# First pairs of an attention: half of one rotation moved to Pool, one to DVE, idle products added, SyncE's order fixed

## The chip, the cores and the metric

The kernel runs on one core of a Trainium2 chip. The core has a matrix engine (PE, with PEld for its weight loads), a vector engine (DVE), a scalar engine (ACT), a general engine (POOL), a queue engine that only issues transfers (SP, SyncE), and 16 DMA engines that carry the transfers. The metric is the device time of one launch in microseconds (us). Before the change it is 1183.55 us, the median of three runs (1183.39 to 1185.93).

## The reference

Three stages follow one another, all in float32:

```
# 1: attention, 2 batches x 8 heads, 576 positions, 64 wide
q, k = rotate(q), rotate(k)                 # x1*cos - x2*sin, x1*sin + x2*cos
attn = softmax(q @ k.T / sqrt(64));  x = attn @ v
# 2: top-1 experts over the 1152 rows of x (512 wide), 8 experts, 1024 hidden
idx = argmax(cosine(x, expert_emb) / tau);  x = gate * relu(x @ w1[idx]) @ w2[idx]
# 3: 8 dense experts, mixed by a matrix P that is normalized 8 times in turn
out = sum_e P[:, e] * (relu(x @ w1[e]) @ w2[e])
```

## The kernel before

The attention works on eight pairs of heads. A pair's q and k lie in one tile `r` (128 partitions: head j = 0 on partitions 0 to 63, head j = 1 on the rest; index x = 0 is q, x = 1 is k). A pair goes through five stations:

- `load_pair` loads `r`, `load_values` loads the values `vr`; both are issued by SP.
- `rotate` multiplies `r` by the table `tb` and adds the two halves: two instructions, on DVE or Pool.
- `split_pair` cuts q or k in a high and a low part: ACT writes the high part into `hl`, Pool subtracts to get the low part, and SP copies both by DMA into `qd` (four transfers of 144 KB) or `kd` (four of 288 KB), where the two parts of one head lie on 128 partitions.
- `scores` multiplies `kd` with `qd` on PE; DVE takes the row maximum `nb`, ACT the exponential `p`.
- `turn`, `values`, `rows` transpose `p`, multiply it with the values and turn the result.

The loop runs in steps k = 0 to 88. A step does the scores of one block of 120 rows (five blocks a head, ten steps a pair), so pair i is first needed at step 10 i. In step 10 (i - 1) + 3 pair i's q is split, in step 10 (i - 1) + 5 its k; only for pair 1 are these steps 8 and 7. The first pair is not split: its scores come straight from the tile `first`, which takes 64 partitions, that is one head, at a time. Its rotation is cut in six instructions a head by `rotate_first`: all of k, then q's columns 0 to 239, then the rest. Before the loop, 30 products of a tile `wz` of ones (`keep_warm`) run on PE; nothing uses them.

SP also issues the first expert's weights for stage 2: `fetch(raw1, w1a, ...)` stands at the head of step 15 and `fetch(raw2, w2a, ...)` at the head of step 55, four transfers of 512 KB each.

`with tc.manual_schedule(engines=ORDERED)` keeps the order of the code on PE, DVE, ACT and Pool. SP is not in `ORDERED` before, so its order is chosen by the scheduler. SP's transfers use eight semaphores in turn: each transfer from the ninth on waits until the one eight places ahead of it has landed. All of them go through one hardware queue (q1).

Of the kernel before, what the change touches and what calls it, by code (L numbers as in the profile page):

```python
# [36 lines left out]
ORDERED = {mybir.EngineType.PE, mybir.EngineType.DVE, mybir.EngineType.Activation, mybir.EngineType.Pool}  # L37
# [10 lines left out]
def fused_kernel(ctx, tc, qk, vv, tab, cst, emb, tau, w1a, w2a, wg, w1b, w2b, out):  # L48
    nc = tc.nc
    V, A, G, T = nc.vector, nc.scalar, nc.gpsimd, nc.tensor  # L50
# [9 lines left out]
    def bank(tag, bufs, name, shape=(128, 512)):  # L60
        return ps[0].tile(list(shape), F32, tag=tag, bufs=bufs, name=name)
# [13 lines left out]
    def fetch(raws, src, n, e, cond=None):  # L75

        ei = slice(e, e + 1) if isinstance(e, int) else bass.ds(e, 1)
        for i, raw in enumerate(raws):
            nc.sync.dma_start(out=raw.rearrange("p (g c) -> p g c", g=n // 128),
                              in_=src[ei, i * n:(i + 1) * n, :].rearrange("o (g p) c -> p (o g) c", p=128),  # L80
                              **({} if cond is None else dict(cond=cond)))
# [4 lines left out]
    cs = rt.tile([128, C_END], F32, name="cs")  # L86
# [12 lines left out]
        for x in (1, 0):  # L99
            nc.sync.dma_start(out=first[half, x], in_=qk[0, 0, half, x])  # L100
    nc.sync.dma_start(out=io, in_=cst[:, :256])
    nc.sync.dma_start(out=cs, in_=cst[:, 256:])
    em = at.tile([E, DM], F32, name="em")
    nc.sync.dma_start(out=em, in_=emb)
    taut = at.tile([128, 1], F32, name="taut")
    nc.sync.dma_start(out=taut, in_=tau.to_broadcast([128, 1]))

    def inv_norm(dst, sq, tmp):

# [21 lines left out]
    def embeddings():  # L131

        esq = at.tile([E, DM], F32, name="esq")
        es = at.tile([E, 4], F32, name="es")
        yield V.tensor_copy(uo[:, :128], cs[:, COLS["u"]])
        yield V.tensor_copy(uo[:, 128:], ones)
        yield A.activation(esq, em, AF.Square, accum_out=es[:, 0:1])
        yield V.reciprocal(taut, taut)
        yield from inv_norm(es[:, 1:2], es[:, 0:1], es[:, 2:3])
        yield V.tensor_tensor(es[:, 1:2], es[:, 1:2], taut[:E], op=ALU.mult)  # L140
        yield V.tensor_scalar_mul(em, em, es[:, 1:2])
        yield
        yield
        p = bank("t", 2, "pe_")
        for c in range(NP):
            T.transpose(p[:, c * E:(c + 1) * E], em[:, c * 128:(c + 1) * 128], ident[:E, :E])
        pv = p[:, :NP * E].rearrange("p (c e) -> p c e", e=E)
        for j in range(2):
            half = slice(j * 64, (j + 1) * 64)
            yield V.tensor_copy(enb[half, :, j, :], pv[half])  # L150
# [14 lines left out]
    wz = at.tile([128, 512], BF16, name="wz")  # L165
    V.memset(wz, 1.0)

    def load_pair(i):
        b, pr = divmod(i, NP)
        r = first  # L170
        if i > 0:
            r = at.tile([128, 2, 2, S], F32, tag="r", bufs=2, name="r")
            nc.sync.dma_start(out=r, in_=qk[b, pr])
        ops[i] = dict(r=r)

    def load_values(i):
        b, pr = divmod(i, NP)
        vr = ops["v", i] = at.tile([QT, NQ, 2, D], F32, tag="vr", bufs=3, name="vr")
        G.memset(vr[96:QT, 4], 0.0)
        nc.sync.dma_start(out=vr[:, 0:4].rearrange("p t h d -> p t (h d)"),  # L180
                          in_=vv[b, pr, 0:480].rearrange("(t p) d -> p t d", p=QT))
        nc.sync.dma_start(out=vr[0:96, 4].rearrange("p h d -> p (h d)"), in_=vv[b, pr, 480:S])
# [6 lines left out]
    def rotate(i, x, eng, rows=slice(0, 128), cols=slice(0, S)):  # L189
        r = ops[i]["r"][rows, x][:, :, cols]  # L190
        eng.tensor_tensor(r, r, tb[rows][:, :, cols], op=ALU.mult)
        eng.tensor_tensor(r[:, 0], r[:, 0], r[:, 1], op=ALU.add)

    def rotate_first(j):

        rows, c, rest = slice(j * 64, (j + 1) * 64), slice(0, 2 * QT), slice(2 * QT, S)
        yield rotate(0, 1, V, rows)
        yield rotate(0, 0, V, rows, c)
        yield rotate(0, 0, V, rows, rest)

    def split_pair(i, x):

# [31 lines left out]
    def exps(n, t, s, nb):  # L234
        i, j = divmod(n, 2)
        m = TW[t]
        A.activation(ppad[n % 2][:m, t, :S].rearrange("p (h n) -> p h n", h=2), s[:m, :, :HS], AF.Exp,  # L237
                     bias=nb[:m], scale=1.0, accum_out=sums[:m, i, t, j:j + 1])
# [28 lines left out]
    def gather_pair(i):  # L267
        A.activation(upad[i % 2][:, :S].rearrange("p (h n) -> p h n", h=2), ops["o", i][:, :, :HS], AF.Copy)
# [9 lines left out]
    def keep_warm(w, n):  # L278

        p = bank("t", 2, "warm")  # L280
        for _ in range(n):
            T.matmul(p, w[:, :128], w[:, :512], start=True, stop=True)
# [149 lines left out]
    def squares(b):  # L432
        for c in range(NQ):
            sq = tmp("sq", [QT, DM], BF16) if (b, c) == (0, 0) else ops["sq"]
            ops["sq"] = sq
            yield A.activation(sq, ops["x", b][:, c], AF.Square, accum_out=nsq[:, b, c:c + 1])
# [37 lines left out]
        V.tensor_copy(idx[:, 1], ig)  # L474

    pairs = B * NP
    for i in range(2):
        load_pair(i)
        load_values(i)
    trickle = embeddings()  # L480
    heads = 2 * pairs

    ahead = {0: 2, 3: 0, 5: 1}
    last = pairs - 1
    with tc.manual_schedule(engines=ORDERED):
        waiting, out_rows, squared = None, None, iter(())
        keep_warm(wz, 30)
        second = rotate_first(1)
        for _ in rotate_first(0):
            pass  # L490
        for k in range(NQ * heads + 9):
            n, t = divmod(k, NQ)
            nt, kt = divmod(k - 6, NQ)
            iv, kv = divmod(k - 12, 2 * NQ)
            if waiting is not None:
                exps(*waiting)
                waiting = None
            if k in (1, 2, 3):
                next(second, None)
            if k >= 7:  # L500
                for _ in range(2 if k < 40 else 1):
                    next(trickle, None)
            if k == 15:
                fetch(raw1, w1a, 128, 0)
            if k == 55:
                fetch(raw2, w2a, 256, 0)
            if out_rows is not None:
                rows_out(*out_rows)
                if out_rows[:2] == (NP - 1, 1):
                    trickle, squared = route_half(0), squares(0)  # L510
                out_rows = None
            next(squared, None)
            if n < heads:
                waiting = (n, t) + scores(n, t)

            if iv >= last:
                kv *= 2
            if 0 <= iv <= last and kv == 9 + (iv == last):
                gather_pair(iv)
            if 0 <= nt < heads:  # L520
                if kt == 0:
                    ops["ph", nt] = at.tile([128, NQ, S], F32, tag="ph", bufs=4, name="ph")[:QT]
                    turn(nt, -1)
                turn(nt, kt)
            if 0 <= iv <= last and kv % 2 == 0 and kv < 2 * NQ:
                if kv == 0:
                    ops["o", iv] = bank("o", 1, "o", (128, 2, 512))
                values(iv, kv // 2)
            if iv == last and kv == 12:
                keep_warm(ops[last]["k"][:, 0, 0], 8)  # L530
                logits_first(last)
                parts = [rows(last, x) for x in range(2)]
            elif 0 < iv <= last and k % (2 * NQ) in (2, 3):
                out_rows = rows((k - 22) // (2 * NQ), k % (2 * NQ) - 2)
            i = k // (2 * NQ) + 1
            if k < 2 * NQ:

                part = {0: 2, 7: 1, 8: 0}.get(k)
                if k == 5:
                    rotate(1, 1, V)  # L540
            else:
                part = ahead.get(k % (2 * NQ))
            if part is not None and i < pairs:
                if part < 2:
                    split_pair(i, part)
                else:
                    room(i)
                    rotate(i, 0, G)
                    if i > 1:
                        rotate(i, 1, G)  # L550
                        load_values(i)
                    if i + 1 < pairs:
                        load_pair(i + 1)
        routes = route_half(1)
        for _ in range(5):
            next(routes)
        for x in parts:
            rows_out(*x)
        next(routes)
# [647 lines left out]
```

## Time and profile before

| what | us |
|---|---|
| median of three runs | 1183.55 |
| the profiled execution's own time | 1185.82 |
| its span, first to last instruction | 1183.70 |
| PE busy in the span | 1146.0 (97%) |
| DVE, ACT, POOL busy | 838.5, 513.9, 144.5 |

The profiled execution took 2.12 us outside its span, and 2.27 us more than the median. The attention's scores begin at 10.88 us, the second pair's at 41.44, the third's at 59.37; the attention's last block ends near 186. From the second pair on PE is nearly always busy.

Times in rows are us from the start of the span. The granted clock of PE (PEclk) is 1.00 at 2.4 GHz and 0.50 at 1.2 GHz. Line numbers are those of the kernel before; the changed file's lines are 3 higher in the functions and the loop.

### The profile page before, as it was taken

Reading aid. Unit: us, or ns where it says so; the run is one execution under the profiler, and the core shown is the slowest. Engines: PE = TensorE matmul, PEld = TensorE weight load, DVE = VectorE, ACT = ScalarE, POOL = GpSimd, SP = SyncE. Lnnn points to the kernel's source line nnn. Section 1 sums busy time; section 2 is a strip of 40 time slices with the busy share of each in tenths; the row PEclk is TensorE's granted clock in tenths of the full one; section 3 lists DMA queues with packets and bytes.
Section 4 is the critical chain, followed back from the end, with each engine's and each line's share of the span. In section 5 each row is a group of like instructions: output and inputs, shape, how many; then the busy total and the mean of one; then the engine's idle time right before and its main releaser. Section 6 shows DMA issues by size and latency. Waiting matters only on the chain.

```text
span 1183.7 us, 17171 instructions
## 1 busy us (share of the span) xinstructions
PE 1146.0 (97%) x6658; PEld 981.4 (83%) x6658; DVE 838.5 (71%) x1293; ACT 513.9 (43%) x788; POOL 144.5 (12%) x95
## 2 busy tenths in 40 slices
PE   8999998999998889999999999999999999999998
PEld 4677776788886768899989998899989998989997
DVE  6776776899996456776676667666766676667665
ACT  2565754788885344323332333333333333333330
POOL 2657403133231200000000000000000000000000
PEclk7799998999999789999999999999999999999999
DMA  7788524355285401111111111111111111111102
GB/s 209 206 239 207 133 54 131 125 177 214 84 293 185 125 19 36 54 54 36 36 54 54 37 36 54 54 36 37 55 54 36 38 53 54 37 40 50 36 1 81
DMA packets 75187, 103.90 MB, mean 88 GB/s; under 512 B 5400, under 2 KB 45336, under 8 KB 74208
## 3 DMA queue, kind: packets, MB, share of 16 engines
q1 hardware_dynamic: 72160, 94.13, 26.7%
q0 software_dynamic: 2368, 7.60, 1.9%
q8 instruction: 53, 0.87, 0.3%
q10 hardware_dynamic: 576, 1.05, 0.2%
q14 instruction: 30, 0.25, 0.1%
HBM read 111.35 MB, written 8.39 MB: 101 GB/s over the span
## 4 chain that ended last, share of the span: by engine, by line
PE 64%; DVE 1%; DMA 1%; issue 1%; ACT 1%; SPq 0%; POOLq 0%
PE o L1062 34%; PE d L1026 29%; DMA g<-yd 1%; PE o L970 0%; DVE yq L897 0%; DMA yd<-y,idx 0%; ACT yq L894 0%; DVE yt L942 0%; PE d L922 0%; PE o L1001 0%; ACT h L1051 0%; DVE st L1041 0%; DVE w L859 0%; ACT w L858 0%; SPq L910 0%
## 5 line engine op out<-in xcount | busy, mean ns | idle before, releaser
L1062 PE MATMUL o<-w,h 128*128 128x512 f32 x1728 | 433.6, 393 | 0.7 <-ACT acc L1066 0.7
L1026 PEld LDWEIGHTS d<-yq,w 128*128 128x128 f32 x2688 | 381.7, 189 | 20.5 <-ACT st L1038 1.0
L1026 PE MATMUL d<-yq,w 128*128 128x288 f32 x2688 | 395.4, 296 | 1.3 <-ACT st L1038 0.7
L1062 PEld LDWEIGHTS o<-w,h 128*128 128x128 f32 x1728 | 312.8, 188 | 55.4 <-ACT acc L1066 1.1
L1073 DVE SCALAR_TENSOR_TENSOR acc<-o,P,acc 128x512 f32<-128x512 f32 x252 | 189.1, 750 | 160.0 <-PE o L1062 160.0
L1051 ACT ACTIVATE h<-st 128x576 fp32r<-128x576 f32 x96 | 65.8, 686 | 223.2 <-DVE st L1041 223.2
L1038 ACT ACTIVATE st<-d 128x576 f32<-128x576 f32 x96 | 62.7, 653 | 221.6 <-PE d L1026 221.6
L572 DVE TENSOR_TENSOR wlo<-raw,whi 128x2048 fp32r<-128x2048 f32 x56 | 127.8, 2288 | 15.8 <-ACT whi L579 15.5
L579 ACT ACTIVATE whi<-raw 128x2048 fp32r<-128x2048 f32 x52 | 99.9, 1920 | 10.9 <-PE h L607 3.5
L1041 DVE TENSOR_TENSOR st<-st,d 128x576 f32<-128x576 f32 x96 | 72.1, 751 | 41.0 <-PE d L1026 41.0
L237 ACT ACTIVATE p<-s,nb 120x576 f32<-120x576 f32 (+1 forms) x80 | 59.1, 739 | 62.5 <-DVE nb L231 52.5
L231 DVE TENSOR_REDUCE nb<-s 120x1 f32<-120x576 f32 (+1 forms) x80 | 60.2, 754 | 35.2 <-PE s L228 18.9
L804 ACT ACTIVATE w<-raw 128x512 fp32r<-128x512 f32 (+1 forms) x128 | 73.3, 573 | 17.3 <-DVE raw L842 14.0
L805 DVE TENSOR_TENSOR w<-raw,w 128x512 fp32r<-128x512 f32 (+1 forms) x128 | 78.9, 617 | 0.0
L1052 DVE SCALAR_TENSOR_TENSOR h<-st,h 128x576 fp32r<-128x576 f32 x96 | 72.0, 750 | 4.8 <-ACT h L1051 4.7
L228 PE MATMUL s<-kd,qd 128*120 128x288 f32 x280 | 55.7, 322 | 3.9 <-DMA qd<-hl 2.6
L228 PEld LDWEIGHTS s<-kd,qd 128*120 128x120 f32 x280 | 39.3, 182 | 16.6 <-issue 10.2
L251 PE MATMUL pt<-io,p 120*120 120x120 f32 x320 | 48.6, 276 | 1.4 <-DVE ph L257 0.3
L634 PE MATMUL y<-whi,hh 128*128 128x512 f32 x112 | 45.7, 408 | 2.2 <-ACT hh L624 2.2
L264 PE MATMUL o<-ph,vr 120*64 120x288 f32 x320 | 47.4, 418 | 0.0
L634 PE MATMUL y<-wlo,hh 128*128 128x512 f32 x112 | 44.2, 394 | 0.0
L257 DVE COPY ph<-pt 120x480 f32<-120x480 f32 x64 | 41.5, 649 | 2.9 <-PE pt L251 2.6
(245 smaller groups left out, 1123.4 us busy)
## 6 DMA issues: line engine op xcount, KB each, us to landing
raw<-w1a SPq DMA_DIRECT2D x56, 512.0 KB
raw<-w2a SPq DMA_DIRECT2D x56, 512.0 KB
raw<-w1b SPq DMA_DIRECT2D x64, 256.0 KB
raw<-w2b SPq DMA_DIRECT2D x32, 512.0 KB
r<-qk SPq DMA_DIRECT2D x7, 1152.0 KB
kd<-hl SPq DMA_DIRECT2D x28, 288.0 KB
qd<-hl SPq DMA_DIRECT2D x28, 144.0 KB
g<-yd SPq DMA_DIRECT2D x4, 576.0 KB
```

The lines of the kernel that those rows point to most:

```text
L228: T.matmul(s[:m, h, :HS], qd[:, j, t * QT:t * QT + m], kd[:, j, x, h * HS:(h + 1) * HS], start=(x == 0), stop=(x == 1))
L572: V.tensor_tensor(lo, raw, hi, op=ALU.subtract)
L579: A.activation(hi, raw, AF.Copy)
L634: T.matmul(p, a[:, kk], b, start=(k == 0 and n == 0), stop=(k == KF - 1 and n == 2))
L804: A.activation(hi, src, Copy)
L805: V.tensor_tensor(lo, src, hi, op=ALU.subtract)
L1026: T.matmul(d[1][:, q, :QW], wv[:, wx, which, k], yq[yx][:, YQ[p], k, q * QW:(q + 1) * QW], start=new and k == 0 and (wx, yx) == (0, 0), st ...
L1041: V.tensor_tensor(halves(st[x]), halves(st[x]), mid(d), op=ALU.add)
L1051: A.activation(hi, src, AF.Relu)
L1052: V.scalar_tensor_tensor(lo, src, 0.0, hi, op0=ALU.max, op1=ALU.subtract)
L1062: T.matmul(d, hs[n][:, r, hx, t * 128:(t + 1) * 128], w2[n][:, wx, r], start=(r == 0 and (hx, wx) == (0, 0)), stop=(r == 1 and hx == 1))
L1073: V.scalar_tensor_tensor(a, d, p, a, op0=ALU.mult, op1=ALU.add)
```

## The change

Four edits, all in the attention:

- The second head of the first pair is rotated by Pool instead of by DVE, whole and ahead of the loop (before, DVE did it in steps 1 to 3). Pool's rotation of pair 1's q goes to DVE: it rotates pair 1's k in step 4 and q in step 5. Pair 1's k is then split in step 6, its q in step 7.
- Pair 1's load stands ahead of the constants `cs`, `em`, `taut` and of the values.
- 28 products of `wz` instead of 30 run before the loop, and three more follow each of the steps 0 to 5 and two each of the steps 6 to 9.
- SP is added to the engines that keep the code's order.

```diff
-    nc.sync.dma_start(out=cs, in_=cst[:, 256:])
     em = at.tile([E, DM], F32, name="em")
-    nc.sync.dma_start(out=em, in_=emb)
     taut = at.tile([128, 1], F32, name="taut")
-    nc.sync.dma_start(out=taut, in_=tau.to_broadcast([128, 1]))
+
+    def load_constants():
+        nc.sync.dma_start(out=cs, in_=cst[:, 256:])
+        nc.sync.dma_start(out=em, in_=emb)
+        nc.sync.dma_start(out=taut, in_=tau.to_broadcast([128, 1]))
...
-    def rotate_first(j):
+    def rotate_first(j, eng):
         rows, c, rest = slice(j * 64, (j + 1) * 64), slice(0, 2 * QT), slice(2 * QT, S)
-        yield rotate(0, 1, V, rows)
-        yield rotate(0, 0, V, rows, c)
-        yield rotate(0, 0, V, rows, rest)
+        rotate(0, 1, eng, rows)
+        rotate(0, 0, eng, rows, c)
+        rotate(0, 0, eng, rows, rest)
...
-    for i in range(2):
-        load_pair(i)
-        load_values(i)
+    load_pair(0)
+    load_pair(1)
+    load_values(0)
+    load_constants()
+    load_values(1)
...
-    with tc.manual_schedule(engines=ORDERED):
+    with tc.manual_schedule(engines=ORDERED | {mybir.EngineType.SP}):
-        keep_warm(wz, 30)
-        second = rotate_first(1)
-        for _ in rotate_first(0):
-            pass
+        keep_warm(wz, 28)
+        rotate_first(0, V)
+        rotate_first(1, G)
...
-            if k in (1, 2, 3):
-                next(second, None)
...
-                part = {0: 2, 7: 1, 8: 0}.get(k)
-                if k == 5:
-                    rotate(1, 1, V)
+                part = {0: 2, 6: 1, 7: 0}.get(k)
+                if k in (4, 5):
+                    rotate(1, 5 - k, V)
+                keep_warm(wz, 3 if k < 6 else 2)
...
                     room(i)
-                    rotate(i, 0, G)
                     if i > 1:
+                        rotate(i, 0, G)
                         rotate(i, 1, G)
```

On SP, from pair 1's split (the first `kd` and `qd`) to pair 2's (the second), before:

```order
L215 DMA kd<-hl 64x2x576 x4
L213 DMA qd<-hl 64x576 x4
L173 DMA r<-qk 128x2304
L79 DMA raw_74<-w1a 128x1024
L79 DMA raw_75<-w1a 128x1024 x2
L213 DMA qd<-hl 64x576 x4
L215 DMA kd<-hl 64x2x576 x4
```

and now:

```order
L218 DMA kd<-hl 64x2x576 x4
L216 DMA qd<-hl 64x576 x4
L183 DMA vr<-vv 120x4x128
L185 DMA vr<-vv 96x128
L176 DMA r<-qk 128x2304
L216 DMA qd<-hl 64x576 x4
L79 DMA raw_74<-w1a 128x1024 x2
L79 DMA raw_75<-w1a 128x1024 x2
L218 DMA kd<-hl 64x2x576 x4
```

The first expert's `w1a`, of which one transfer was issued ahead of pair 1's `kd` and three ahead of pair 2's `qd`, now goes out as four transfers between pair 2's `qd` and its `kd`. On SP, around the split of pair 6 (steps 53 to 55), before:

```order
L329 DMA xd<-x 120x3x128
L213 DMA qd<-hl 64x576 x4
L329 DMA xd<-x 120x128
L332 DMA xd<-x 96x128
L215 DMA kd<-hl 64x2x576 x4
```

and now:

```order
L332 DMA xd<-x 120x3x128
L216 DMA qd<-hl 64x576 x4
L332 DMA xd<-x 120x128
L335 DMA xd<-x 96x128
L79 DMA raw_76<-w2a 128x2x512 x2
L79 DMA raw_77<-w2a 128x2x512 x2
L218 DMA kd<-hl 64x2x576 x4
```

The four `w2a` transfers, which before stood in twos ahead of the `qd` of pairs 3 and 4, now stand between `qd` and `kd` of pair 6. On DVE, from the end of the first head's rotation to the first copy of a transposed block, now:

```order
L195 TENSOR_TENSOR first<-first 64x336
L234 TENSOR_REDUCE nb<-s 120x1 x4
L234 TENSOR_REDUCE nb<-s 96x1
L194 TENSOR_TENSOR r<-r,tb 128x1152
L195 TENSOR_TENSOR r<-r 128x576
L234 TENSOR_REDUCE nb<-s 120x1
L194 TENSOR_TENSOR r<-r,tb 128x1152
L195 TENSOR_TENSOR r<-r 128x576
L234 TENSOR_REDUCE nb<-s 120x1
L260 COPY ph<-pt 120x480
```

Before, the second head's six instructions stood in pairs between the first four of these maxima, and only one pair of `r` instructions followed, after the sixth maximum. On Pool, from its first rotation to the first split, now:

```order
L194 TENSOR_TENSOR first<-first,tb 64x1152
L195 TENSOR_TENSOR first<-first 64x576
L194 TENSOR_TENSOR first<-first,tb 64x2x240
L195 TENSOR_TENSOR first<-first 64x240
L194 TENSOR_TENSOR first<-first,tb 64x2x336
L195 TENSOR_TENSOR first<-first 64x336
L209 TENSOR_TENSOR hl<-r,hl 128x576 x2
```

Before, two instructions on pair 1's `r` stood where these six on `first` stand now.

## Rows read from the trace of the kernel before

**Rows 1.** Windows (us, busy by engine, PEclk, DMA share, GB/s): attention's steady part

```profile
42.00:186.00 144.00, 141.23 (x1062) 106.70 (x1061) 104.89 (x206) 85.68 (x201) 63.00 (x41) 0.99 0.63 166
```

**Rows 2.** Timeline of PE (start, length, line, out<-in, count, idle before and releaser)

```profile
7.08 3.86 PE L282 MATMUL warm<-wz 128*128 128x512 bf16 x17
...
10.88 2.20 PE L224 MATMUL s<-first 64*120 64x288 f32 x8
...
23.32 4.19 PE L224 MATMUL s<-first 64*120 64x288 f32 x8 [2.34 <-ACT p L237]
...
41.44 1.29 PE L228 MATMUL s<-kd,qd 128*120 128x288 f32 x4 [2.63 <-DMA qd<-hl]
...
59.37 0.78 PE L228 MATMUL s<-kd,qd 128*120 128x288 f32 x4
...
136.06 0.76 PE L228 MATMUL s<-kd,qd 128*120 128x288 f32 x4 [0.36 <-issue]
```

**Rows 3.** Windows around changes of PE's clock

```profile
13.96:41.27 27.31, 21.72 (x53) 12.04 (x53) 18.70 (x27) 10.15 (x24) 9.83 (x6) 0.50 0.67 190
41.27:44.68 3.41, 3.24 (x15) 3.23 (x16) 1.84 (x4) 0.83 (x2) 3.41 (x2) 0.50 0.98 360
...
208.50:211.90 3.40, 0.89 (x6) 0.66 (x7) 3.19 (x5) 3.40 (x5) 0.00 (x0) 1.00 0.12 43
211.90:215.35 3.45, 3.45 (x12) 2.78 (x10) 3.45 (x4) 0.93 (x2) 0.00 (x0) 0.51 0.00 0
```

**Rows 4.** Timeline of DVE, first pair and pair 1's rotation

```profile
12.14 0.76 DVE L231 TENSOR_REDUCE nb<-s 120x1 f32<-120x576 f32 x1 [0.50 <-PE s L224]
...
18.70 2.90 DVE L192 TENSOR_TENSOR first<-first 64x336 f32<-64x336 f32 x1
...
26.48 1.36 DVE L191 TENSOR_TENSOR r<-r,tb 128x1152 f32<-128x1152 f32 x1
27.88 0.76 DVE L192 TENSOR_TENSOR r<-r 128x576 f32<-128x576 f32 x1
```

**Rows 5.** Timeline of POOL, pair 1's rotation of q and its first split

```profile
18.63 2.60 POOL L191 TENSOR_TENSOR r<-r,tb 128x1152 f32<-128x1152 f32 x1 [14.01 <-DMA r<-qk]
...
30.82 1.41 POOL L206 TENSOR_TENSOR hl<-r,hl 128x576 fp32r<-128x576 f32 x1 [7.95 <-ACT hl L205]
```

**Rows 6.** Waits of SP's queue, 0 to 145 us (in total, times, longest)

```profile
SPq L173 <- DMA first<-qk: 1.3, 1, 1.3
```

**Rows 7.** Timeline of ACT: an exponential, a copy, a split

```profile
12.94 0.74 ACT L237 ACTIVATE p<-s,nb 120x576 f32<-120x576 f32 x1 [10.90 <-DVE nb L231]
...
28.53 0.57 ACT L255 ACTIVATE ph<-pt 120x480 f32<-120x480 f32 x1 [1.21 <-PE pt L246]
...
30.07 0.67 ACT L205 ACTIVATE hl<-r 128x576 fp32r<-128x576 f32 x1
```

**Rows 8.** Timeline of SP's issues

```profile
11.65 0.35 SPq L173 DMA_DIRECT2D r<-qk  x1
...
32.25 3.88 SPq L215 DMA_DIRECT2D kd<-hl  x4
...
40.80 1.68 SPq L79 DMA_DIRECT2D raw<-w1a  x3
...
49.87 3.33 SPq L213 DMA_DIRECT2D qd<-hl  x4
53.44 3.77 SPq L215 DMA_DIRECT2D kd<-hl  x4
...
129.68 0.40 SPq L332 DMA_DIRECT2D xd<-x  x1
130.71 3.86 SPq L215 DMA_DIRECT2D kd<-hl  x4
```

**Rows 9.** Windows: DMA rate while pair 1's split, then while the weights are moved

```profile
34.00:42.00 8.00, 5.37 (x16) 2.89 (x15) 3.91 (x7) 2.69 (x6) 5.00 (x3) 0.50 0.98 223
42.00:48.70 6.70, 6.70 (x47) 5.86 (x46) 5.58 (x13) 3.07 (x7) 4.59 (x4) 0.80 0.97 387
```

## The prediction

> **What bounds the kernel now.** I began with busy time by stretch. From the second pair to the attention's end PE is busy 141.23 of 144.00 us at a granted clock of 0.99 [rows 1]: there every microsecond in which PE waits is lost, and every one saved ahead of it comes out at the end. So only PE's timeline matters, and on it the places where PE waits or runs slowly [rows 2]. Step 0 begins at 10.88, pair 1 (step 10) at 41.44: ten steps in 30.56 us, though two steps of scores take 2.20 us at the start. Two things stretch them. The clock: from 13.96 to 41.27 it is granted at 0.50, the 1.2 GHz level, and returns only at 44.68 [rows 3]; two steps of scores then take 4.19 [rows 2]. And the wait for pair 1's data: step 10 stands 2.63 us for `qd`. At step 20 (59.37) PE waits for nothing, at step 60 (136.06) it has 0.36 us with no transfer named [rows 2]. The reader should keep these two in mind: they are where pairs 2 and 6 are first needed, and the change moves transfers just ahead of them.
>
> **The change, part by part.**
>
> *Start of step 0.* The 17 products from 7.08 to 10.88 take 0.22 us each [rows 2]; two fewer start step 0 at 10.44.
>
> *Steps 0 to 5.* At the full clock a step costs PE 1.10 of scores (half of 2.20) and 3 x 0.22 of products, 1.76 us. DVE's maximum (0.76) and ACT's exponential (0.74) fit beside it [rows 4, 7]. DVE no longer rotates between them. Step 4 begins at 17.48, its maximum ends near 19.4, step 5 can begin at 19.24.
>
> *The second head on Pool.* Pool takes 2.60 us for 1152 elements and 1.41 for 576 [rows 5], so 0.22 plus 2.07 ns an element: the six instructions (1152, 576, 480, 240, 672, 336 elements) take 8.5 us. Their data has landed at 11.65, when SP was released by the fourth `first` load [rows 6, 8]; DVE has just finished the first head (free from 11.64, [rows 4]). Pool is then through the columns that step 5 needs at 17.6, and through all at 20.1. Step 5 doesn't wait for it.
>
> *Pair 1's rotation on DVE.* It is ready at 19.4, but a DVE instruction with two inputs in SBUF has to wait for Pool: the addition at 18.70, which took 0.50 for the other head, took 2.90 while Pool multiplied from 18.63 to 21.23 [rows 4, 5]. So it starts at 20.1: 1.36 + 0.76 for k, to 22.2, and step 5's maximum to 23.0. Then ACT's exponential 0.74, copy 0.57, split 0.67 [rows 7], Pool's subtraction 1.41 [rows 5], and 0.4 for four hand-offs (an estimate; the one that the rows show, 12.90 to 12.94, is shorter): SP can issue `kd` at 26.9 instead of 32.25. From there to step 10 the trace has 9.19 us (32.25 to 41.44, [rows 8, 2]), all of it transfer, at 223 GB/s and a DMA share of 0.98 [rows 9]. Step 10 begins at 36.1, a gain of 5.3. Without any waiting for Pool it would be 0.7 more; with Pool and DVE taking turns between the two pieces about 1 less. Pair 1's load has landed by 18.63 already now [rows 5], before DVE could use it, so its place ahead of the constants gains nothing; the constants have time until step 7.
>
> *The clock at step 10.* PE would be ready some 4 us before `qd` is. Today the clock rose 3.24 us after step 10 began [rows 2, 3], a stretch of work with hardly a gap. After the change I take 5 us at 1.2 GHz, a loss of 0.9 more; bounds 0 and 1.8.
>
> *Weights in front of `kd`, pair 2.* This is what SyncE's order costs. Before, `w1a` went out ahead of `qd` and was done: 42.00 to 48.70 ran at 387 GB/s [rows 9], `qd` came at 49.87, `kd` at 53.44 [rows 8]. Now four times 524,288 bytes stand between them; at 387 GB/s that is 5.4 us. How long `kd` needs on an empty queue is seen at pair 6: issued at 130.71, used at 136.06, 5.35 us later [rows 8, 2]. For pair 2 this gives 58.79, against 59.37: slack 0.6. All `w1a` lies in the queue (the issue ahead of it ends at 53.20, three take 1.68) before `kd`, so `kd` comes 5.4 late and PE waits 4.8 at step 20. SP's own 2.2 us for four issues lie inside the 5.4. The 40.80 rows speak for a queue served in order: `w1a`, issued while `qd` was still moving, left the rate at 223 until 42, and the 387 came after it [rows 8, 9].
>
> The Trainium skill, "DMA: Bandwidth & Descriptors", section "Queues, rings and completion order", says the same against this change: on each DMA engine the descriptors of one issuer's queue are consumed in ring order. By it the sum stays; by even sharing among all that is outstanding it would be C's, below. The 387 that follows the 223 agrees with the page.
>
> *Weights in front of `kd`, pair 6.* `w2a` is issued from 130.08, when the last `xd` is out, and `kd` was issued at 130.71 [rows 8], so 0.6 of the 5.4 is over before; slack is nought to 0.3. I take 4.5; bounds for each of the two waits 2.0 and 6.0.
>
> *The clock after these waits.* The nearest gap is that of 208.50 to 211.90, where PE is busy 0.89 us; the next 3.45 us run at 0.51 [rows 3], which loses 1.7. PE's two waits are longer, so 1.7 each; bounds 0 (the slow stretch falls into the wait) and 3.4 (two such stretches).
>
> Sum: -5.3 + 0.9 + 4.8 + 1.7 + 4.5 + 1.7 = +8.3 us. On the profiled execution (1183.70 span, 1185.82 in all) that is 1194.1; it lies 2.27 above the median, and the forecast for the median is 1183.55 + 8.3 = 1191.9. The edits past step 60 change nothing, and the other stages shift as a whole.
>
> **The rivals.**
>
> *A, the weights don't hold up `kd`.* If the engines serve `kd` beside the weights at no cost, or its slack is larger than I read, only the start counts: -5.3 + 0.9 = -4.4, 1179.2, faster. For it: the DMA share in the attention is only 0.63 on the mean [rows 1], and `kd` moves at half the rate of the weights, so the engines might overlap them. Against it: the share is 0.97 to 0.98 where transfers are outstanding, whatever their rate [rows 9]. It decides if `kd` comes less than 2 us late.
>
> *B, the clock falls in the first ten steps all the same.* PE was busy 21.72 of 27.31 us from 13.96 to 41.27 and stayed at 0.50 [rows 3]; the same scores run after the change, and the products may not hold the clock. Then they cost time: a product takes 0.44 at 1.2 GHz (twice 0.22), and steps 2 to 9 need 21.72 + 20 x 0.44 = 30.5 us of PE, so step 10 begins near 44.5, 3.0 later than before. With the four later terms, 12.7, that is +15.7, 1199.3. Against it: with 0.66 of full-array work in 1.76 us PE has no gap until step 6.
>
> The Trainium skill, "TensorE: Matmul & The Clock Gate", section "What's actually happening", has activity release a throttle that is there by default. Read plainly, that excludes B, and the sum stays at +8.3; the row, with PE busy 21.72 of 27.31 us and the clock at 0.50 all the time, does not bear it out, and by it B stays open at +15.7.
>
> *C, half of the weights' delay, no loss of clock.* If engines share evenly among what is outstanding, `kd` of the first head (two transfers, 590 KB, 2.6 us at 223 GB/s) takes twice as long beside the weights and comes 2.6 late. Waits of 2.0 and 2.3 with the start's -4.4 leave -0.1: 1183.5, no change. For it: nothing but that the rows show no landing times; against it: the step from 223 to 387.
>
> **How the numbers follow.** Chances: forecast 0.55, A 0.20, B 0.12, C 0.13. The forecast's own range, from the bounds of its terms, is 1186 to 1197. A measurement of this kernel tells about 0.2% (2.4 us) from no change. Faster takes A and a quarter of C and a little of the forecast's tail: 0.25; the same takes half of C and the tail's rest: 0.10; slower 0.65. The range must hold the half of A nearer to the kernel before and half of B: 1179 to 1199.
>
> **What would show it.** Right: Pool's six instructions on `first` from about 11.7, each as long as its elements say; PEclk 1.00 until step 6 or so; `kd` issued near 27 and step 10 near 36 with a wait for `qd`; a wait of 4 to 5 us for `kd` at step 20 and at step 60, each with PEclk 0.50 behind it; the attention's end 8 us later than before. Wrong: step 20 or step 60 beginning without a transfer named in the wait (then A), or PEclk 0.50 from step 2 on (then B). A start of step 5 that waits for Pool would put the error in Pool's time.

## The result, and the profile after

The changed kernel takes 1197.54 us (median of four runs, 1196.82 to 1200.78) where the kernel before took 1183.47 beside it: ratio 1.0121, 95% interval 1.0107 to 1.0134. It is slower by 14.07 us, the forecast said 8.3. The two profiled executions differ by 11.1 (1196.96 against 1185.82); the rest is where each lies about its median, 2.35 above for before, 0.58 below for after.

The waits of PE in the attention after the change, 0 to 200 us (in total, times, longest):

```profile
PE s L231 <- DMA kd<-hl: 15.1, 3, 8.0
PE s L231 <- DMA qd<-hl: 4.2, 1, 4.2
```

The chain that was to be read is all there: one wait for pair 1's `qd`, and two long ones for a `kd`. The timeline of PE after (start, length, line, out<-in, count, idle before and releaser) puts them in place. These are steps 0, 10, 19, 20, 23, 59, 60 and 63, against [rows 2]:

```profile
9.77 1.23 PE L227 MATMUL s<-first 64*120 64x288 f32 x4 [0.45 <-DVE first L195]
...
35.37 1.22 PE L231 MATMUL s<-kd,qd 128*120 128x288 f32 x4 [4.19 <-DMA qd<-hl]
...
52.20 0.77 PE L231 MATMUL s<-kd,qd 128*96 128x288 f32 x4
...
60.22 1.29 PE L231 MATMUL s<-kd,qd 128*120 128x288 f32 x4 [6.83 <-DMA kd<-hl]
...
69.53 0.77 PE L231 MATMUL s<-kd,qd 128*120 128x288 f32 x4
...
137.11 0.77 PE L231 MATMUL s<-kd,qd 128*96 128x288 f32 x4
...
146.53 1.29 PE L231 MATMUL s<-kd,qd 128*120 128x288 f32 x4 [7.96 <-DMA kd<-hl]
...
155.39 0.79 PE L231 MATMUL s<-kd,qd 128*120 128x288 f32 x4
```

Set against the same steps of before, the account runs like this:

| step | before | after | difference | what came in |
|---|---|---|---|---|
| 0 | 10.88 | 9.77 | -1.11 | first loads, fewer products |
| 10 | 41.44 | 35.37 | -6.07 | the start |
| 19 | 58.24 | 52.20 | -6.04 | |
| 20 | 59.37 | 60.22 | +0.85 | wait for `kd`, 6.9 |
| 23 | 66.53 | 69.53 | +3.00 | slow clock, 2.15 |
| 59 | 134.24 | 137.11 | +2.87 | (a wait of 0.93 for `kd` at step 50 is gone) |
| 60 | 136.06 | 146.53 | +10.47 | wait for `kd`, 7.6 |
| 63 | 142.65 | 155.39 | +12.74 | slow clock, 2.3 |
| 79 | 172.25 | 185.00 | +12.75 | |
| end of span | 1183.70 | 1194.80 | +11.10 | |

So the start gave 6 us, the two waits took 14.5 and the clock behind them 4.4. The later stages take 1.65 back. By the trace's record of the granted clock they ran at 0.50 for 34.1 us before and for 27.3 after, which is enough to make up the difference; that it is the cause isn't shown.

Windows of after (us, busy by engine, PEclk, DMA share, GB/s): the first ten steps, the head of pair 1, the wait at step 20, and the slow stretches at steps 20 and 60.

```profile
4.72:35.44 30.72, 25.33 (x110) 12.13 (x107) 22.06 (x30) 10.97 (x26) 19.02 (x12) 1.00 0.82 212
35.44:38.85 3.41, 3.41 (x17) 3.37 (x18) 2.06 (x5) 0.83 (x2) 1.30 (x2) 0.50 0.90 210
...
49.40:60.20 10.80, 3.99 (x33) 2.95 (x32) 4.68 (x9) 2.95 (x7) 6.16 (x4) 0.80 1.01 278
55.92:66.16 10.24, 5.94 (x25) 4.27 (x26) 1.77 (x3) 1.48 (x3) 0.20 (x1) 0.50 0.51 112
141.25:151.49 10.24, 4.96 (x19) 3.31 (x20) 1.49 (x3) 1.48 (x3) 0.67 (x2) 0.50 0.49 101
```

The first row answers to [rows 3]: the clock that had been 0.50 from 13.96 on is now 1.00 up to step 10, for which PE has waited 4.19 us. The third says that the DMA engines were at work for the whole wait. The last two show 10.24 us at 1.2 GHz each, of which PE works the last six and five: the slow stretch outlasts the wait.

SP's issues after (start, length, line, out<-in, count), against [rows 8]:

```profile
26.25 3.86 SPq L218 DMA_DIRECT2D kd<-hl  x4
...
47.26 2.02 SPq L79 DMA_DIRECT2D raw<-w1a  x4
49.38 3.33 SPq L218 DMA_DIRECT2D kd<-hl  x4
...
132.96 1.97 SPq L79 DMA_DIRECT2D raw<-w2a  x4
135.03 2.58 SPq L218 DMA_DIRECT2D kd<-hl  x4
```

Pair 1's `kd` goes out 6.00 us earlier than before (26.25 against 32.25). The `kd` of pairs 2 and 6 goes out behind the weights, and 2.07 to 2.12 us after the first of them.

### The profile page after: what moved, and what is told of

It is laid out like the page before. It is cut to its first block, busy times and chain, and to the rows that moved or that the text cites. A ratio compares the mean times of both kernels' runs of the same rounds, so it can differ in the third digit from the quotient of the medians.

```text
span 1194.8 us, 17216 instructions
## 1 busy us (share of the span) xinstructions
PE 1142.5 (96%) x6682; PEld 977.2 (82%) x6682; DVE 835.2 (70%) x1289; ACT 513.3 (43%) x788; POOL 148.8 (12%) x99
## 4 chain that ended last, share of the span: by engine, by line
PE 63%; DVE 1%; issue 1%; DMA 1%; ACT 1%; SPq 0%; POOLq 0%
PE o L1065 33%; PE d L1029 29%; DMA g<-yd 1%; PE o L973 0%; DVE yq L900 0%; DMA yd<-y,idx 0%; ACT yq L897 0%; PE d L925 0%; DVE yt L945 0%; PE o L1004 0%; ACT h L1054 0%; DVE st L1044 0%; ACT yt L787 0%; DVE w L862 0%; ACT w L861 0%
## 5 line engine op out<-in xcount | busy, mean ns | idle before, releaser
L240 ACT ACTIVATE p<-s,nb 120x576 f32<-120x576 f32 (+1 forms) x80 | 59.1, 738 | 74.0 <-DVE nb L234 62.4
```

## The experiments

Ratios are to the kernel before, run beside the kernel on the same chip, with 95% intervals.

### The weights behind `kd`

```diff
-            if k == 15:
-                fetch(raw1, w1a, 128, 0)
-            if k == 55:
-                fetch(raw2, w2a, 256, 0)
...
                     if i + 1 < pairs:
                         load_pair(i + 1)
+            if k == 15:
+                fetch(raw1, w1a, 128, 0)
+            if k == 55:
+                fetch(raw2, w2a, 256, 0)
```

> The changed kernel with both fetches moved from the head of steps 15 and 55 to their end, so that SP issues the same four transfers right behind kd instead of right ahead of it. Theory (one queue served in order): the waits of 6.9 and 7.6 us at steps 20 and 60 go, total 1176 to 1180, like the early weights. Rival (transfers outstanding together share the engines evenly): kd is still slowed by the weights beside it, waits of 3 to 5 us remain at both steps, total 1185 to 1192.

Measured: 1177.60 us (six runs), ratio 0.9952 (0.9934 to 0.9971). The same transfers in the same steps, issued after `kd` instead of ahead of it, turn +14 us into -6. Step 20 begins at 53.65, after 0.28 us with no transfer named; step 60 waits for 0.40, in this row of PE's timeline:

```profile
129.76 0.77 PE L231 MATMUL s<-kd,qd 128*120 128x288 f32 x4 [0.40 <-DMA kd<-hl]
```

Its `kd` was issued here, by SP's timeline:

```profile
124.37 3.83 SPq L218 DMA_DIRECT2D kd<-hl  x4
```

That is 5.39 us from issue to use with nothing ahead, and this time PE did wait, so it is the transfer's own time; the forecast had taken 5.35 from before. While the weights move behind `kd` no longer wait arises: even sharing among all that is outstanding (C) falls.

### The weights early

The fetch is cut up: one transfer of `w1a` in step 1, three in step 12, and `w2a` in twos in steps 22 and 32, about where they stood before; SP's order stays fixed. `only` picks among a fetch's four transfers.

```diff
-            if k == 15:
-                fetch(raw1, w1a, 128, 0)
-            if k == 55:
-                fetch(raw2, w2a, 256, 0)
+            if k in (1, 12):
+                fetch(raw1, w1a, 128, 0, only=(0,) if k == 1 else (1, 2, 3))
+            if k in (22, 32):
+                fetch(raw2, w2a, 256, 0, only=(0, 1) if k == 22 else (2, 3))
```

> The changed kernel with the expert weights issued ahead of qd: one w1a transfer in step 1, three in step 12, two of w2a in step 22, two in step 32; SP stays in order. Theory (weights between qd and kd are what costs): step 10 near 35.4 as in the changed kernel, step 20 near 53.3 and step 60 near 130 with a wait for kd under 1 us, clock 1.00 there, the attention 6 us earlier than in the kernel before, total 1176 to 1179. Rival (SP's fixed order itself, with vr ahead of r, makes kd late): waits of several us remain at step 20 or 60 and the total stays above 1190.

Measured: 1179.36 us (twelve runs), ratio 0.9963 (0.9950 to 0.9977), within 0.4 of the range expected. The waits for `kd` shrink to 1.2 us in all, in this answer on PE's waits:

```profile
PE s L233 <- DMA qd<-hl: 4.2, 1, 4.2
...
PE s L233 <- DMA kd<-hl: 1.2, 3, 0.5
```

Two places as far apart as these give the same gain, so it isn't when the weights move that counts, but that they don't stand ahead of a `kd` which PE is about to need.

### SP's order alone

The kernel before, with the fourth edit only:

```diff
-    with tc.manual_schedule(engines=ORDERED):
+    with tc.manual_schedule(engines=ORDERED | {mybir.EngineType.SP}):
```

> The kernel before with one edit alone, SP added to the engines in the code's order. Theory: step 10 at 41.4 as before, then the waits at steps 20 and 60 with the slow clock behind them, each 9 to 10 us in all: 1200 to 1204. Rival (the waits come from the new start, with kd and qd issued in a tighter row): no wait over 2 us at steps 20 and 60, total 1183 to 1186.

Measured: 1200.63 us (four runs), ratio 1.0148 (1.0114 to 1.0183). Both waits are there without any of the other edits:

```profile
PE s L228 <- DMA kd<-hl: 13.1, 2, 6.8
```

The order alone is to blame, and the rest of the change is a gain. One thing was missed: step 10 begins at 38.28, not at 41.4. The one `w1a` that stood ahead of pair 1's `kd` before isn't the reason: it had landed by 25.25, and `kd` went out at 32.25. The reason stands on DVE. Before, the last addition for the second head began at 18.70, just behind Pool's multiplication at 18.63, and took 2.90 [rows 4, 5]; in this execution it began just ahead of Pool's:

```profile
18.04 0.51 DVE L192 TENSOR_TENSOR first<-first 64x336 f32<-64x336 f32 x1
```

```profile
18.25 2.77 POOL L191 TENSOR_TENSOR r<-r,tb 128x1152 f32<-128x1152 f32 x1 [13.63 <-DMA r<-qk]
```

The maximum behind it starts 3.07 us earlier (first row: before; second: this run):

```profile
21.64 1.42 DVE L231 TENSOR_REDUCE nb<-s 120x1 f32<-120x576 f32 x2
```

```profile
18.57 0.76 DVE L231 TENSOR_REDUCE nb<-s 120x1 f32<-120x576 f32 x1
```

With it `kd` goes out 3.06 earlier (29.19). A few tenths of a microsecond decide this, so some 3 of the 6 us at the start may be owed to the one execution of the kernel before that was profiled.

### Half of the weights ahead

First two transfers ahead of `kd` and two behind it; then two ahead of `kd` and the other two eleven steps later, so that nothing follows `kd` either. Shown is `w1a`; `w2a` is treated alike in step 55.

```diff
-                fetch(raw1, w1a, 128, 0)
+                fetch(raw1, w1a, 128, 0, only=(0, 1))
...
+            if k == 15:
+                fetch(raw1, w1a, 128, 0, only=(2, 3))
```

> The changed kernel with two of the four weight transfers of steps 15 and 55 left ahead of kd and two moved behind it. Theory (a queue in order, each transfer ahead of kd costs its own time): at the 1.35 us per transfer that the forecast took, kd is 2.7 late and the waits are near 2.1 and 1.9; at the 1.9 to 2.1 that the changed kernel's waits give (6.9 + 0.6 and 7.6 + 0.3, over four), 3.2 and 3.6. The clock falls behind one or both. Total 1183 to 1189. Rival (a fixed penalty as soon as weights stand between qd and kd): waits stay near 7, total near 1197.

Measured: 1191.15 us (four runs), ratio 1.0054 (1.0036 to 1.0072). The total lies between the two forecasts, and the waits, 5.2 and 5.7, are longer than the theory's:

```profile
PE s L233 <- DMA kd<-hl: 10.9, 2, 5.7
```

```diff
-            if k == 15:
-                fetch(raw1, w1a, 128, 0)
+            if k in (15, 26):
+                fetch(raw1, w1a, 128, 0, only=(0, 1) if k == 15 else (2, 3))
```

and the same for `w2a` in steps 55 and 66.

> The changed kernel with two of the four weight transfers ahead of kd at steps 15 and 55, the other two put off to steps 26 and 66, so that nothing stands behind kd. With two behind kd the waits were 5.3 and 5.7. Theory (each transfer ahead costs 1.9, those behind disturb kd as well): waits of 3 to 4 us, total 1184 to 1188. Rival (a fixed loss of some 3.5 us as soon as weights and kd follow one another, whatever is behind): waits stay at 5 to 6, total 1190 to 1192.

Measured: 1190.00 us (five runs), ratio 1.0050 (1.0030 to 1.0071); waits 9.9 us in all, 4.9 each. The theory's 3 to 4 us is out; the total is the rival's, the waits lie just under its 5 to 6. So it isn't what follows `kd`. By the two rows of SP and PE that belong together, from `kd`'s issue to its use it takes:

| weights ahead | kernel | pair 2 | pair 6 |
|---|---|---|---|
| none | weights behind `kd` | - | 5.39 |
| two | two ahead, two far behind | 9.90 | 9.50 |
| two | two ahead, two behind | 10.18 | 10.17 |
| four | SP's order alone | 10.41 | 9.84 |
| four | the change | 10.84 | 11.50 |

From `kd`'s issue, the first two transfers cost 4.5 us (mean 9.94 less 5.39), the next two 0.7 (mean 10.65). By 387 GB/s [rows 9] it would be 2.7 for each two. The sum for four is as the rate says; the way to it isn't. Part of that is the way of counting: the second two also put off `kd`'s issue by 1 us. From the issue of the first weights to the use of `kd` it takes 11.07 with two and 12.75 with four (means), which is 5.7 and 7.4 more than with none.

The other part is in the end of the wait. The trace has 16 landing events for each transfer, taken here as one for each DMA engine; the step needs the second `kd` copy whole. Its middle landing comes 4.8 us after `kd`'s issue with no weights ahead (pair 6 of the kernel before, and of the one with the weights behind), 7.7 with two and 9.4 with four (means of four each). That is 2.9 for the first two, close to the rate, and 1.8 for the next, with the 1 us of issue 2.7. But the last landing comes 0.35 after the middle one with none, 2.1 with two and 1.0 with four (and 1.4 in pair 2 with the weights behind, where step 20 begins right after it). In this run's pair 2, fifteen have landed by 57.36 and the last at 59.00; step 20 begins at 59.29. The windows show the same:

```profile
57.00:58.00 1.00, 0.00 (x0) 0.00 (x0) 0.00 (x0) 0.00 (x0) 0.00 (x0) 0.96 0.68 177
58.00:59.00 1.00, 0.00 (x0) 0.00 (x0) 0.00 (x0) 0.00 (x0) 0.00 (x0) 0.50 0.16 51
```

PE does nothing, and the 16 DMA engines are 0.68 and then 0.16 busy: PE waits for a late one. It was late already in the weights: fifteen landings of the first `w1a` are in by 52.10, the sixteenth at 54.84. At 51.23 the trace has a packet of 16 KB on queue q8 ("instruction") that took 2.35 us; but pair 6 of the change has a late landing (1.65 behind the fifteenth) without such a packet beside it. Why one engine falls behind the weights stays open.

### Products in the two waits

The change as it is, with 33 products of `wz` ahead of the scores of steps 20 and 60, where PE would stand still:

```diff
+            if k in (20, 60):
+                keep_warm(wz, 33)
```

> The changed kernel with 33 more unused products ahead of the scores of step 20 and of step 60, some 7.1 us of work on PE at the full clock, in the time in which it waits for kd. Theory (each wait costs its own length, 6.9 and 7.6, and the slow clock behind it 2.2 more): kd lands when it did, the clock stays at 1.00 after both steps, total 4 to 5 us under the changed kernel, near 1193. Rival (the slow clock lies within the wait and costs nothing, the rest of the loss comes from elsewhere): the clock stays up and the total is that of the changed kernel, 1197, or higher.

Measured: 1192.20 us (six runs), ratio 1.0074 (1.0054 to 1.0094), 5.3 less than the change. In PE's timeline the products fill the wait:

```profile
55.95 7.28 PE L285 MATMUL warm<-wz 128*128 128x512 bf16 x32 [1.06 <-DVE ph L260]
62.88 0.89 PE L231 MATMUL s<-kd,qd 128*120 128x288 f32 x4
```

and the clock stays at 2.4 GHz through both of them (window of the attention from step 12 on):

```profile
41.60:205.50 163.90, 155.81 (x1142) 113.14 (x1142) 107.13 (x223) 90.66 (x208) 58.36 (x37) 1.00 0.55 145
```

Steps 20 to 23 take 6.71 instead of 9.31 us and steps 60 to 63 take 6.60 instead of 8.86: 2.6 and 2.3, 4.9 in all. So about 5 of the change's loss is the clock behind the waits, and the rest the waits. The profiled execution alone would not show it: there the clock was back only at 41.63 after step 10 (with the change 38.85), `kd` went out 1.52 later, and step 20 began 2.66 later, so that step 79 is 2.15 earlier (182.85 against 185.00). That the products are worth 5 rests on the steps' lengths and on the medians.

### Pair 1's place in the load order

The weights behind `kd`, and the constants ahead of pair 1's load as before the change:

```diff
-    load_pair(0)
-    load_pair(1)
-    load_values(0)
-    load_constants()
+    load_constants()
+    load_pair(0)
+    load_values(0)
+    load_pair(1)
     load_values(1)
```

> The changed kernel with the weights behind kd and the loads of the start back in the old order: constants, values of pair 0, pair 1, values of pair 1. Theory (pair 1's load is not on the path): it lands by 18.7, before DVE turns to it at 19.4, step 10 at 35.6 as with pair 1 ahead, total 1177 to 1178.5. Rival (DVE finds it late): rotation of k from 20 on or later, step 10 at 37 or later, total 1179 to 1181.

Measured: 1178.44 us (five runs), ratio 0.9952 (0.9935 to 0.9970), the ratio of the kernel with the weights behind `kd`. Step 10 begins at 35.06, there at 35.62. The edit gains nothing.

### No products in the first ten steps

The weights behind `kd`, without the 26 products in steps 0 to 9:

```diff
-                keep_warm(wz, 3 if k < 6 else 2)
```

> The changed kernel with the weights behind kd and without the 26 products of the first ten steps; the 28 ahead of the loop stay. Theory (the products hold the clock): PEclk falls to 0.50 between 11 and 18 as in the kernel before, two steps of scores take 4.2, step 10 begins at 37 to 40 instead of 35.6, total 1179 to 1183. Rival (the clock falls from the waits between steps of the kernel before, which the change removes anyway, so products do nothing): clock 1.00 to step 9, step 10 at 35 to 36, total 1177 to 1178.

Measured: 1180.10 us (five runs), ratio 0.9957 (0.9943 to 0.9971). The clock falls as it did before:

```profile
14.00:41.30 27.30, 25.75 (x77) 16.72 (x76) 16.68 (x29) 11.87 (x29) 18.66 (x13) 0.50 0.71 198
```

The total is the theory's, but step 10 begins at 35.98 and not at 37 to 40, with 1.55 us of waiting for `qd` left: at 1.2 GHz PE just about keeps up with the transfers. Step 20 is 1.15 later (54.80 against 53.65), as the clock comes back late. The products hold the clock, and holding it is worth little as long as pair 1's copies are later than PE.

### Products alone

The kernel before, with only the 28, three and two products:

```diff
-        keep_warm(wz, 30)
+        keep_warm(wz, 28)
...
+                keep_warm(wz, 3 if k < 6 else 2)
```

> The kernel before with one edit alone, the products: 28 instead of 30 ahead of the loop, three after each of the steps 0 to 5, two after each of the steps 6 to 9. Theory (clock and pair 1's chain both count): the clock stays at 1.00 until step 9, but DVE still rotates the second head and pair 1's k waits for it, so step 10 begins at 37 to 39, 2.5 to 4.5 earlier than before, total 1179 to 1181. Rival (the gain comes from moving the rotations, products alone only lengthen PE's steps): step 10 at 41 or later, total 1183 to 1187.

Measured: 1181.42 us (ten runs), ratio 0.9983 (0.9967 to 0.9998). PE's clock is 1.00 through the first steps, then PE waits and it falls:

```profile
6.10:33.40 27.30, 24.43 (x103) 11.74 (x103) 22.82 (x33) 11.03 (x26) 8.79 (x5) 1.00 0.84 223
33.40:43.60 10.20, 6.17 (x29) 5.99 (x29) 4.46 (x11) 2.13 (x5) 6.19 (x5) 0.50 0.97 317
```

Step 10 begins at 37.43, four earlier than before, after 6.09 us of waiting for `qd`. The products don't account for all four: here too DVE's last addition for the second head began ahead of Pool's multiplication (18.62), and the maximum behind it starts 3.35 earlier than before (18.29 against 21.64):

```profile
17.75 0.51 DVE L192 TENSOR_TENSOR first<-first 64x336 f32<-64x336 f32 x1
```

Against the kernel with SP's order alone, which has no such collision either, `kd` goes out 0.86 earlier (28.33 against 29.19). Most of what the clock gives is waited away.

### Products ahead of step 10

The weights behind `kd`, and the wait at step 10 filled:

```diff
+            if k == 10:
+                keep_warm(wz, 18)
```

> The changed kernel with the weights behind kd and 18 more unused products (3.9 us at the full clock) ahead of the scores of step 10, in the wait of 4.3 us for qd. Theory (a PE that waits 4 us works on at 1.2 GHz for 3.4 us and loses 1.7): the clock stays at 1.00 from about 5 to past 180, step 10 still near 35.5, step 20 some 1 to 1.7 us earlier, total 1176 to 1177, within the measurement of 1177.6 for the weights behind kd alone. Rival (the products hold up step 10 or cost more than they save): step 10 later than 36, total 1178 to 1180.

Measured: 1175.53 us (five runs), ratio 0.9925 (0.9911 to 0.9938). Step 10 begins no earlier (35.71), but runs at the full clock, as everything from 6.60 to 184.10 does:

```profile
6.60:184.10 177.50, 172.79 (x1214) 122.89 (x1214) 129.28 (x247) 100.67 (x230) 79.35 (x50) 1.00 0.66 174
```

Step 20 begins at 52.36, 1.29 earlier than with the wait left empty.

### The first head's copies first

As the last one, with seven products at step 10 in place of 18; and of pair 1's eight copies, the four of head 0 (`kd`, then `qd`) go out ahead of those of head 1:

```diff
...
+        if i == 1:
+            for what, j in ((1, 0),) if x == 1 else ((0, 0), (1, 1), (0, 1)):
+                put(what, j)
...
```

Here `put(what, j)` issues the two copies of one head, `what` being 0 for `qd` and 1 for `kd`.

> The changed kernel with the weights behind kd, pair 1's eight copies reordered (kd of head 0, qd of head 0, kd of head 1, qd of head 1 instead of all kd, all qd) and 7 unused products ahead of step 10 instead of 18. Theory (from SP's first kd issue to step 10 all is transfer, and step 10 needs only head 0): two kd copies, 2.8 us, go behind what step 10 waits for, so step 10 begins at 32.7 to 33.2 instead of 35.7, the clock stays at 1.00, total 1172 to 1174. Rival (SP's issues or Pool's subtraction of q bind, not the transfers): step 10 at 34.5 or later, total 1175 or more.

Measured: 1174.37 us (six runs), ratio 0.9924 (0.9904 to 0.9943), the lowest time here, though not to be told from the one above. Step 10 begins 2.71 earlier and waits for no transfer, which shows that its start was set by the bytes ahead of it. Half of that is lost again two steps later (step 12 at 36.84, with the copies as before 38.27):

```profile
33.00 0.76 PE L238 MATMUL s<-kd,qd 128*120 128x288 f32 x4
...
36.45 0.63 PE L261 MATMUL pt<-io,p 120*120 120x120 f32 x4 [1.32 <-DVE es L118]
```

The new wait is for DVE, which is late with the maxima of steps 10 and 11. In DVE's timeline of this kernel a small instruction for the experts' embeddings, 8x1 elements, takes 2.57 us while Pool multiplies beside it (32.51 to 35.15), and the maximum of step 10 comes only behind it, though its scores began at 33.00:

```profile
32.59 2.57 DVE L117 TENSOR_TENSOR es<-es 8x1 f32<-8x1 f32 x1
35.09 0.74 DVE L241 TENSOR_REDUCE nb<-s 120x1 f32<-120x576 f32 x1
```

## Why the prediction came out as it did

The direction, the mechanism and its places were right; the size was 5.8 us short. The time lies in the range given, 1179 to 1199, but 0.5 above the forecast's own, 1186 to 1197. What held it is the part that was added for rival B, which didn't happen: that is luck. The own range was also narrower than its terms' bounds, which add up to 1182 to 1199. Both waits came out above their bound of 6.0. The terms, with what they measured:

| term | forecast | measured |
|---|---|---|
| start of step 10 | -5.3 | -6.1 |
| clock at step 10 | +0.9 | 0.0 |
| wait at step 20 | +4.8 | +6.9 |
| clock behind it | +1.7 | +2.15 |
| wait at step 60 | +4.5 | +7.6 |
| clock behind it | +1.7 | +2.3 |

The measured terms make 12.9 in the two profiled executions, 4.6 more than the forecast. The later stages took 1.65 of that back, and the medians lie 2.9 further apart than the two executions.

**The step that failed** is "SP's own 2.2 us for four issues lie inside the 5.4". From `kd`'s issue on, the working holds: 5.35 and 5.4 make 10.75, measured were 10.84 for pair 2 (49.38 to 60.22) and 11.50 for pair 6. But `kd` also goes out later. Before, it was issued 4.80 us ahead of step 19 (53.44 to 58.24), now 2.82 ahead (49.38 to 52.20): 1.98 lost, what SP needs for the weights. Then 1.98 + (10.84 - 5.39) - 0.54 of slack (59.37 less 53.44 and 5.39) = 6.89, the wait that is seen. For pair 6 the lead over step 59 falls from 3.53 to 2.08: 1.45, and 11.50 - 5.39 = 6.11 make 7.56. There the forecast had moreover taken 0.6 off for weights that would be through before `kd`'s issue; none were.

That 10.75 came out is partly luck. It was worked out as bytes over a rate; with half the bytes ahead the cost was 4.5 us and not 2.7, as the last engine came later still. A queue in order was right: in the change's trace the middle landings of pair 2 follow the order of issue, the four `w1a` at 50.9, 52.3, 54.2 and 56.4, the first two `kd` at 57.9 and 59.1. By the rule of the Trainium skill, "DMA: Bandwidth & Descriptors", section "Queues, rings and completion order", that on each DMA engine the descriptors of one issuer's queue are consumed in ring order, the trace agrees as to the order: `kd` came in behind the weights both times, and on time when it was issued ahead of them.

**The clock** behind the waits cost 2.15 and 2.3 in place of 1.7. The price had been taken from a gap of 3.40 us with 3.45 us of slow work after it [rows 3]; after the longer gaps PE works five to six microseconds at 1.2 GHz. The estimate's upper bound of 3.4 held. The price isn't fixed: by the same steps (20 to 23, 60 to 63) it was 1.2 and 2.1 with SP's order alone, 1.3 and 2.8 with two ahead and two behind.

**The start.** Step 10 came 0.7 earlier than forecast (35.37 against 36.1). Step 0 was 0.67 early (9.77 against 10.44): it waited for DVE's rotation, whose data landed earlier in this execution, and not for the products. But a step then took 1.91 and not 1.76, and step 4 began at 17.42, forecast 17.48. What was won came behind pair 1's rotation: step 5's maximum ended at 22.78 (forecast 23.0), and from there to `kd`'s issue it took 3.47, of which the forecast's pieces are 3.39, so the hand-offs were 0.1 in all and not 0.4 (its pieces, moreover, add up to 26.8 and not 26.9). On Pool the six instructions on `first` begin at 11.91 (forecast 11.7) and end at 21.5, as the POOL timeline shows (its first and last):

```profile
11.91 2.60 POOL L194 TENSOR_TENSOR first<-first,tb 64x1152 f32<-64x1152 f32 x1 [7.30 <-DMA first<-qk]
...
19.56 1.95 POOL L195 TENSOR_TENSOR first<-first 64x336 f32<-64x336 f32 x1
```

The forecast had DVE wait for Pool to the end (20.1); in fact they took turns, which it had priced at about 1 us of the gain, and against waiting to the end that cost nothing. DVE's multiplication began at 19.41 and took its full 1.34. Pool's last instruction, begun at 19.56, took 1.95, by its elements 0.92, so some 1.0 of it is waiting, to DVE's end at 20.75. DVE's addition then took 1.33 where [rows 4] have 0.76, and ended at 22.12 (forecast 22.2):

```profile
19.41 1.34 DVE L194 TENSOR_TENSOR r<-r,tb 128x1152 f32<-128x1152 f32 x1
20.79 1.33 DVE L195 TENSOR_TENSOR r<-r 128x576 f32<-128x576 f32 x1
```

`kd` went out at 26.25, forecast 26.9, and step 10 came 9.12 us later, forecast 9.19. The products alone and the copies in another order both say that this stretch is all transfer. The claim that pair 1's place in the load order gains nothing held.

**The clock at step 10** was to cost 0.9 more than before. The clock is back 3.48 us after step 10 began, before it was 3.24, and step 19 is 6.04 earlier where step 10 was 6.07: nothing.

**The rivals.** A needed steps 20 and 60 without a transfer named; both name `kd`. B needed PEclk 0.50 from step 2 on; it is 1.00 to 35.44. B's ground was sound all the same: the same scores without the products, PE busy 25.75 of 27.30 us, leave the clock at 0.50; the products decide. The rule of the Trainium skill, "TensorE: Matmul & The Clock Gate", section "What's actually happening", that activity releases the throttle, would not have led one to expect that row. C needed waits near 2; they were 6.9 and 7.6, and with the weights behind `kd` 0.4 in all is left.

## What to carry to other kernels

When a queue engine's order is fixed by hand, place every bulk prefetch behind the small transfers that the matrix engine needs next: the same bytes in the same steps were worth 20 us by which side of `kd` they stood on. Price a transfer behind others from its own issue and add the issue time of what stands ahead; half the bytes needn't be half the delay. Where a wait of several microseconds can't be removed, fill it with products that nothing uses: the slow clock lasts beyond the wait, here by five to six microseconds, and filling the wait gave back 2.3 to 2.6 us each time.

## What the runs showed of the hardware that was not expected

- Two transfers of 512 KB ahead of the `kd` copies delay them by 4.5 us from their own issue, four by 5.3. The last of 16 landings comes 2.1 and 1.0 after the middle one, with nothing ahead 0.35; at the end of the wait the DMA share is 0.16.
- Scores on 64 partitions in float32 left the clock at 0.50 with PE busy 25.75 of 27.30 us; the same scores with two or three bf16 products in each step ran at 1.00 to step 10, though PE was busy for only 25.33 of 30.72 us.
- Gaps of 6.8 and 8.0 us each brought 10.24 us at 1.2 GHz, about half of them after the wait; gaps of 6.4 and 6.8 with SP's order alone brought 6.83 each.
- DVE's addition of 64x336 took 2.90 us when it began 0.07 behind Pool's multiplication, and 0.51 when it began 0.21 ahead of it; with it step 10 moved by 3 us.
- An instruction of 8x1 elements on DVE took 2.57 us beside Pool's work, and by that came to hold up PE when the transfers no longer did.
